# Fewer scratch buffers for a casting DMA, and a reordered weight preparation, in a gated recurrence followed by a max-out layer

## The chip, the cores and the metric

The kernel runs on one core of one Trainium2 chip. The metric is the device time of one execution in microseconds (us). Times of one kernel agree within about 0.3% most of the time. A few executions are much longer; those are marked slow (over 1.5% above the fastest of the same kernel), and every comparison here uses the fast runs alone. A ratio is the mean time of one kernel's fast runs over the mean of the other's fast runs of the same rounds, so it is not quite the ratio of the medians that are quoted beside it.

Engines: PE is TensorE's matmuls, PEld its weight loads, DVE is VectorE, ACT is ScalarE, POOL is GpSimd, SP is SyncE. SPq is the queue in which SP issues DMAs.

## The reference

Two parts run one after the other. The first is a gated recurrence over time for 4 sequences of 6144 steps with 256 features:

```python
sig = 1.0 / (1.0 + np.exp(-f_logit))
f = lower_bound + (1.0 - lower_bound) * sig
h = 0
for t in range(S):
    h = f[:, t] * h + (1.0 - f[:, t]) * x[:, t]
    y[:, t] = h
```

The second takes the 24576 rows of `y` through a layer with two branches, 1024 hidden units each, and a maximum between them:

```python
h1 = y @ w1
h2 = y @ w2
out = np.maximum(h1, h2) @ w_out
```

## The kernel before

The kernel uses `max(h1, h2) = h1 + relu(h2 - h1)`. So the first layer is one product with the difference `wd = (w2 - w1)`, a relu, and the second layer adds `y @ (w1 @ w_out)`. The product `w1 @ w_out`, called `w13`, is made once at the start, for which `w1` has to be transposed on TensorE. All of it is scaled by `om = 1 - lower_bound`, because the kernel leaves that factor out of the recurrence.

Time is cut into 48 blocks of 512 steps. For each block the features must lie on the partitions, so the inputs are transposed. The first chunks are transposed on TensorE. From chunk 5 on (`f`) and 6 on (`x`) it is done by DMA: POOL issues a DMA that casts a chunk of 1024 steps from float32 in DRAM to a bfloat16 scratch buffer, also in DRAM, and SP issues a DMA transpose from there into SBUF.

```python
NSCR = 6
...
            elif by_xbar(c, s):
                scr = scratch[s][uses[s] % NSCR]
                uses[s] += 1
                nc.gpsimd.dma_start(out=scr..., in_=src...)      # cast, DRAM to DRAM
...
                nc.sync.dma_start_transpose(out=dst[:, :, 0:nt], in_=held[c, s][0:nt, :])
...
LEAD_FETCH = 10
LEAD_CROSS = 3
```

A cast may overwrite a scratch buffer only when the transpose that reads it is done, so the number of buffers is the number of casts per tensor that can run ahead. POOL has little else to do and runs ahead as far as it may.

The weights before (with cuts):

```python
        make_w1s(0); make_w1s(1)          # ACT: w1s = om * w1, four times 512 strided columns
        ...
        make_wd(0)                        # DVE: wd = om * w2 - w1s
        for fc in range(0, NQ):
            first_layer(0, fc)            # PE: dT = wd.T @ y; ACT: rt = relu(dT)
        ...
        make_wd(1)
        make_w1T(0); make_w1T(1)          # PE: transpose w1s; ACT: copy to w1T
        for fc in range(NQ, FC):
            first_layer(0, fc)
        make_w1T(2); make_w1T(3)
        make_w13()                        # PE: w1T.T @ w_out; ACT: copy
```

## Time and profile before

The median was 408.92 us in the rounds of the comparison (408.33 to 409.08). The numbers that matter:

| Reading | Value |
|---|---|
| span of the profiled execution | 405.9 us |
| PE busy | 388.1 us, 96% of the span |
| one block in the steady state | 7.82 us |
| all waits of PE | 11.5 us, six of them, in five groups |
| wait of PE in the middle of the work | 1.2 us, at 64 us |

The busy times are the first part of the page of the kernel before (busy us, share of the span, instructions):

```profile
PE 388.1 (96%) x2792; PEld 297.3 (73%) x2840; DVE 247.2 (61%) x345; ACT 273.4 (67%) x446; POOL 28.0 (7%) x59
```

The list of waits of PE in the kernel before (engine, line, what it waited for, microseconds in total, times, longest):

```profile
PE dT L313 <- DVE wd L273: 5.6, 2, 5.2
PE tT L155 <- DVE fn L101: 2.8, 1, 2.8
PE dT L392 <- DVE ident L381: 1.6, 1, 1.6
PE dT L313 <- ACT rt L321: 1.2, 1, 1.2
PE tT L155 <- DVE xn L101: 0.3, 1, 0.3
```

PE is the bound, and only the head of the kernel and one wait at 64 us leave it idle. The wait at 64 us is put down to `rt`, a relu on ACT. The timelines of the kernel before, first of the SP queue, then of ACT, then of PE, show what stood behind it (start, length, engine, line, operation, tiles, and in brackets the idle time before and what ended it):

```profile
30.05 13.82 SPq L365 DMA_DIRECT2D out_dram<-osb  x2
43.97 17.55 SPq L128 DMA_TRANSPOSE fT<-scr_0_90  x1
```

```profile
63.63 1.06 ACT L165 ACTIVATE u<-fT 128x1024 bf16<-128x1024 bf16 x1 [2.65 <-DMA fT<-scr_0_90]
```

```profile
65.22 0.59 PE L313 MATMUL dT<-y,wd 128*128 128x512 bf16 x2 [1.24 <-ACT rt L321]
```

The first DMA transpose sat 17.55 us in the SP queue and landed 19.6 us after its issue (the chain of waits has it as one piece from 43.97 us). ACT's sigmoid waited for it, the relus wait behind the sigmoid in ACT's queue, and PE waits for a relu to free a PSUM buffer.

The head is the other part. PE's timeline before, from the first layer of block 0 to the end of `w13`:

```profile
14.05 3.17 PE L313 MATMUL dT<-y,wd 128*128 128x512 bf16 x7 [0.42 <-DVE wd L273]
17.01 1.25 PE L287 MATMUL psO<-ident_f,w1s 128*128 128x128 f32 x8
18.09 1.98 PE L313 MATMUL dT<-y,wd 128*128 128x512 bf16 x8
19.91 1.03 PE L287 MATMUL psO<-ident_f,w1s 128*128 128x128 f32 x8
20.79 2.41 PE L297 MATMUL psO<-wob,w1T 128*128 128x256 bf16 x16
23.03 0.61 PE L155 MATMUL tT<-ident,fn 128*128 128x128 bf16 x8
```

What comes after 23.03 us is the transposes of block 1, so 23.0 us is the end of the head's weight work on PE.

### The profile page before, as it was taken

The numbers are of one execution on the slowest core, as the hardware profiler recorded it, in microseconds if no ns is written. First come the engines' busy times: TensorE is split into PE (matmuls) and PEld (weight loads), VectorE is DVE, ScalarE is ACT, GpSimd is POOL, SyncE is SP. The second block draws the span as 40 slices with busy tenths as digits, with TensorE's granted clock in tenths as the row PEclk, the third lists the DMA queues.
The fourth block names the chain that finished last, engine by engine and source line by source line (L and its number), as shares of the span: only waits on it lengthen the run. The fifth ranks groups of instructions, "written<-read, shape, count | busy, mean of one in ns | idle before, by whom it ended". The sixth has DMA issues, their size and how long they took to land.

```text
span 405.9 us, 7061 instructions
## 1 busy us (share of the span) xinstructions
PE 388.1 (96%) x2792; PEld 297.3 (73%) x2840; DVE 247.2 (61%) x345; ACT 273.4 (67%) x446; POOL 28.0 (7%) x59
## 2 busy tenths in 40 slices
PE   3699998999999999999999999999999999999996
PEld 2386776777777777777777777777777777777775
DVE  3557665676566567566656656756665665676641
ACT  2948655766766766676676677667667667766762
POOL 0721000000000000000000000000000000000000
PEclk9999999999999999999999999999999999999999
DMA  7999999997999999897997995989772662752212
GB/s 254 206 214 234 247 206 299 210 258 171 233 174 226 205 186 221 195 214 205 206 207 180 234 209 169 237 164 211 155 157 90 170 144 77 195 131 77 105 53 103
DMA packets 97568, 75.43 MB, mean 186 GB/s; under 512 B 87280, under 2 KB 87792, under 8 KB 96880
## 3 DMA queue, kind: packets, MB, share of 16 engines
q1 hardware_dynamic: 93984, 49.56, 47.7%
q0 software_dynamic: 3264, 25.17, 34.2%
q8 instruction: 22, 0.36, 0.4%
q10 hardware_dynamic: 288, 0.26, 0.2%
q14 instruction: 10, 0.08, 0.1%
HBM read 53.48 MB, written 46.66 MB: 247 GB/s over the span
## 4 chain that ended last, share of the span: by engine, by line
PE 82%; DMA 14%; issue 1%; SPq 0%; POOL 0%; ACT 0%; DVE 0%; ACTq 0%
PE psO L342 49%; PE dT L313 34%; DMA fT<-scr_0_90 5%; DMA scr_0_90<-in_f_logit_dram 4%; DMA scr_4_94<-in_f_logit_dram 3%; DMA w1n_118<-in_moe_w_dram 2%; DMA fn<-in_f_logit_dram 1%; POOL waited L269 0%; SPq L97 0%; ACT rt L321 0%; POOL wob L398 0%; SPq L380 0%; SPq L259 0%; DVE osb L351 0%; PE tT L155 0%
## 5 line engine op out<-in xcount | busy, mean ns | idle before, releaser
L321 ACT ACTIVATE rt<-dT 128x512 bf16<-128x512 f32 x384 | 223.3, 598 | 109.5 <-PE dT L313 93.4
L342 PE MATMUL psO<-wob,rt 128*128 128x256 bf16 x1536 | 229.1, 273 | 0.2
L313 PE MATMUL dT<-y,wd 128*128 128x512 bf16 x720 | 218.5, 382 | 6.9 <-DVE wd L273 5.6
L342 PEld LDWEIGHTS <-rt 128*128 128x128 bf16 x1536 | 170.0, 113 | 40.7
L362 DVE COPY osb<-psO 128x512 f32<-128x512 f32 x94 | 64.8, 691 | 76.2 <-PE psO L342 76.0
L208 DVE TENSOR_TENSOR_SCAN y<-ff,y,v 128x512 bf16<-128x512 bf16 x88 | 107.8, 1266 | 0.0
L313 PEld LDWEIGHTS <-wd 128*128 128x128 bf16 x768 | 73.9, 98 | 15.9 <-DVE wd L273 6.4
L342 PE MATMUL psO<-w_117,y 128*128 128x256 bf16 x384 | 73.3, 273 | 2.3
L342 PEld LDWEIGHTS <-y 128*128 128x128 bf16 x384 | 43.3, 113 | 41.0 <-issue 0.3
L195 DVE TENSOR_TENSOR v<-u,xT 128x1024 bf16<-128x1024 bf16 x40 | 27.7, 692 | 55.0 <-ACT u L165 55.0
L165 ACT ACTIVATE u<-fT 128x1024 bf16<-128x1024 bf16 x42 | 44.1, 1051 | 2.7 <-DMA fT<-scr_0_90 2.7
L184 DVE TENSOR_SCALAR ff<-u,nom 128x512 bf16<-128x512 bf16 x96 | 29.3, 347 | 0.0
L195 DVE TENSOR_TENSOR v<-u,tT 128x1024 bf16<-128x1024 bf16 x8 | 9.7, 1218 | 16.2 <-ACT u L165 14.9
L165 ACT ACTIVATE u<-tT 128x1024 bf16<-128x1024 bf16 x6 | 6.2, 1039 | 7.6 <-PE tT L155 7.5
L208 DVE TENSOR_TENSOR_SCAN y<-ff,v 128x512 bf16<-128x512 bf16 x8 | 9.3, 1206 | 0.0
L155 PE MATMUL tT<-ident,xn 128*128 128x128 bf16 x64 | 8.6, 230 | 0.3 <-DVE xn L101 0.3
L155 PE MATMUL tT<-ident,fn 128*128 128x128 bf16 x48 | 5.1, 234 | 2.8 <-DVE fn L101 2.8
L155 PEld LDWEIGHTS <-fn 128*128 128x128 bf16 x48 | 3.9, 105 | 3.5 <-DVE fn L101 3.1
L155 PEld LDWEIGHTS <-xn 128*128 128x128 bf16 x64 | 5.4, 103 | 0.6 <-DVE xn L101 0.6
L106 POOL DMA_DIRECT2D scr_0_90<-in_f_logit_dram x4 | 2.0, 496 | 50.0 <-DMA fT<-scr_0_90 49.4
L106 POOL DMA_DIRECT2D scr_2_92<-in_f_logit_dram x4 | 1.9, 487 | 37.0 <-DMA fT<-scr_2_92 36.2
L106 POOL DMA_DIRECT2D scr_1_91<-in_f_logit_dram x4 | 2.0, 495 | 36.4 <-DMA fT<-scr_1_91 35.8
(41 smaller groups left out, 49.4 us busy)
## 6 DMA issues: line engine op xcount, KB each, us to landing
out_dram<-osb SPq DMA_DIRECT2D x47, 512.0 KB, 3.6
scr_0_90<-in_f_logit_dram POOLq DMA_DIRECT2D x4, 512.0 KB, 6.9
scr_1_91<-in_f_logit_dram POOLq DMA_DIRECT2D x4, 512.0 KB, 6.2
scr_0_96<-in_x_dram POOLq DMA_DIRECT2D x4, 512.0 KB, 8.1
scr_2_92<-in_f_logit_dram POOLq DMA_DIRECT2D x4, 512.0 KB, 7.8
scr_1_97<-in_x_dram POOLq DMA_DIRECT2D x4, 512.0 KB, 8.4
scr_3_93<-in_f_logit_dram POOLq DMA_DIRECT2D x3, 512.0 KB, 6.7
scr_2_98<-in_x_dram POOLq DMA_DIRECT2D x3, 512.0 KB, 9.1
```

The costliest lines, as they stand in the source:

```text
L106: nc.gpsimd.dma_start(out=scr[0:nt, :].rearrange("(p i) d -> p (i d)", p=P), in_=src.rearrange("(p i) d -> p (i d)", p=P),)
L155: nc.tensor.transpose(dst, src, ident[:])
L165: nc.scalar.activation(out=like(u[:, :, 0:nb], src), in_=src, func=AF.Sigmoid, scale=-1.0)
L184: nc.vector.tensor_scalar(out=ff[:, h, 0:nb], in0=u[:, h, 0:nb], scalar1=nom[:, h : h + 1], scalar2=1.0, op0=ALU.mult, op1=ALU.add,)
L195: nc.vector.tensor_tensor(out=like(v[:, :, 0:nb], src), in0=like(u[:, :, 0:nb], src), in1=src, op=ALU.mult,)
L208: nc.vector.tensor_tensor_scan(out=y[:, h, 0:nb], data0=ff[:, h, 0:nb], data1=v[:, h, 0:nb], initial=init, op0=ALU.mult, op1=ALU.add,)
L313: nc.tensor.matmul(dT[:, 0:nb], lhsT=wd[:, kc, fc * P : (fc + 1) * P], rhs=y[:, kc, 0:nb], start=(kc == 0), stop=(kc == KC - 1),)
L321: nc.scalar.activation(out=rt[:, 0:nb], in_=dT[:, 0:nb], func=AF.Relu)
L342: nc.tensor.matmul(ps[:, r, :], lhsT=left, rhs=right, start=(s == 0 and (r == 0 or j == NBLK - 1)), stop=(s == n - 1 and (r == 1 or j == N ...
L362: nc.vector.tensor_copy(out=osb[:, 2 * g : 2 * g + 2, :], in_=ps[:])
```

## The change

The intent has three parts, which are named in what follows. The *queue part*: two scratch buffers per tensor and a shorter fetch lead, so that casts run at most two chunks ahead. The *weights part*: raw `w1` is transposed as soon as it lands, DVE makes the difference and evicts the transposes, ACT only scales. The *hoist*: in block 2 all of `second_layer(1)` goes ahead of the first layer. The core of the diff, with cuts and added comments:

```diff
-    NSCR = 6
+    NSCR = 2
-    LEAD_FETCH = 10
+    LEAD_FETCH = 7
...
+            ahead("cross", cross, j + LEAD_CROSS)
             ahead("fetch", fetch, j + LEAD_FETCH)
-            ahead("cross", cross, j + LEAD_CROSS)
...
+    def make_wd(k):
+        nc.vector.tensor_tensor(out=pair(wdf, k), in0=half(w2n, g)[:, :, qs],
+            in1=half(w1n, g)[:, :, qs], op=ALU.subtract)
         for kc in range(KC):
+            nc.scalar.mul(wd[:, kc, cols], wdf[:, kc, cols], om[:, kc : kc + 1])
...
+        pts = [turn_w1(0), turn_w1(1)]    # PE transposes of raw w1
+        make_wd(0)
         make_wd(1)
+        for fc in range(0, 2):
+            first_layer(0, fc)
+        keep_w1T(0, pts[0])               # DVE evicts
+        make_wd(2)
...
+            if j == 2:
+                for fc in range(FC):
+                    second_layer(1, fc)
             for fc in range(FC):
                 if j < NBLK:
                     first_layer(j, fc)
-                second_layer(j - 1, fc)
+                if j > 2:
+                    second_layer(j - 1, fc)
```

Two smaller edits of the diff are not shown. As raw `w1` is transposed, `om` is multiplied in when ACT evicts `w13`. And the scans of block 2 now come after the first layer of block 1 instead of before it.

More of the change, by code (lines that the diff above doesn't have):

```diff
@@ L238 @@
     wob = wpool.tile([P, FC, D], BF16)
-    w1s = wpool.tile([P, KC, DFF], FP32)
+    wdf = wpool.tile([P, KC, DFF], FP32)
     wd = wpool.tile([P, KC, DFF], BF16)
@@ L262, in fetch_w, with pair, turn_w1 @@
             )
-    def make_w1s(g):
-        for kc in range(KC):
-            nc.scalar.mul(fcs(w1s, kc, g), half(w1n, g)[:, kc], om[:, kc : kc + 1])
     def pool_waits(t):
         nc.gpsimd.tensor_copy(out=waited[:], in_=t)
-    def make_wd(g):
-        for kc in range(KC):
-            nc.vector.scalar_tensor_tensor(
-                out=fcs(wd, kc, g),
-                in0=half(w2n, g)[:, kc],
-                scalar=om[:, kc : kc + 1],
-                in1=fcs(w1s, kc, g),
-                op0=ALU.mult,
-                op1=ALU.subtract,
-            )
-    def make_w1T(k):
+    def pair(w, k):
+        return w[:, :, 2 * k * P : 2 * k * P + 2 * P].rearrange(
+            "p kc (q m) -> p kc q m", q=2
+        )
+    def make_wd(k):
+        g, r = divmod(k, NQ // 2)
+        qs = slice(2 * r, 2 * r + 2)
+        nc.vector.tensor_tensor(
+            out=pair(wdf, k), in0=half(w2n, g)[:, :, qs], in1=half(w1n, g)[:, :, qs],
+            op=ALU.subtract,
+        )
+        cols = slice(2 * k * P, 2 * k * P + 2 * P)
+        for kc in range(KC):
+            nc.scalar.mul(wd[:, kc, cols], wdf[:, kc, cols], om[:, kc : kc + 1])
+    def turn_w1(k):
+        g, r = divmod(k, NQ // 2)
         pt = ps_o.tile([P, KC, 2, P], FP32, name="psO")
@@ L285, in make_w1T, with keep_w1T @@
             for q in range(2):
-                fc = 2 * k + q
                 nc.tensor.transpose(
-                    pt[:, kc, q, :], w1s[:, kc, fc * P : (fc + 1) * P], ident_f[:]
+                    pt[:, kc, q, :], half(w1n, g)[:, kc, 2 * r + q], ident_f[:]
                 )
+        return pt
+    def keep_w1T(k, pt):
         dst = w1T[:, 2 * k : 2 * k + 2, :].rearrange("p q (k d) -> p k q d", k=KC)
-        nc.scalar.copy(out=dst, in_=pt[:])
+        nc.vector.tensor_copy(out=dst, in_=pt[:])
     def make_w13():
@@ L303, in make_w13 @@
                 )
-            nc.scalar.copy(out=w13[:, kc, :], in_=psw[:, 0, :])
+            nc.scalar.mul(w13[:, kc, :], psw[:, 0, :], om[:, kc : kc + 1])
     rts = {}
@@ L394 @@
         recurrence(0)
-        make_w1s(0)
-        make_w1s(1)
         pool_waits(w1n[0][:, 0, 0:1])
@@ L402 @@
         pool_waits(w2n[1][:, 0, 0:1])
-        make_wd(0)
-        for fc in range(0, NQ):
-            first_layer(0, fc)
         fetch(1)
@@ L409 @@
         ahead("fetch", fetch, LEAD_FETCH)
+        pts = [turn_w1(0), turn_w1(1)]
+        make_wd(0)
         make_wd(1)
-        make_w1T(0)
-        make_w1T(1)
-        for fc in range(NQ, FC):
+        for fc in range(0, 2):
             first_layer(0, fc)
-        make_w1T(2)
-        make_w1T(3)
+        keep_w1T(0, pts[0])
+        make_wd(2)
+        for fc in range(2, 4):
+            first_layer(0, fc)
+        make_wd(3)
+        keep_w1T(1, pts[1])
+        pts = [turn_w1(2), turn_w1(3)]
+        for fc in range(4, 6):
+            first_layer(0, fc)
+        keep_w1T(2, pts[0])
+        for fc in range(6, 8):
+            first_layer(0, fc)
+        keep_w1T(3, pts[1])
         make_w13()
@@ L422 @@
         turn(turn_steps(2))
-        recurrence(2)
+        gate(2)
         for fc in range(FC):
             first_layer(1, fc)
+        for step in scan_steps(2):
+            step()
         turn(turn_steps(3))
```

## The prediction

> **What bounds the kernel now.** TensorE. The page gives PE 388.1 of 405.9 us busy, at a granted clock of 1.0; the chain of waits is 82% PE, and the list of waits shows only five waits of PE, 11.5 us in total, all in the first 14 us but for 1.2 us at 64 us, for `rt`. From about 65 us on, the timeline repeats every 7.82 us per block without a PE wait, and PE is busy 49.7 of 50 us in every later stretch, whether DMA share is above 1.0 (100-150 us) or 0.58 (300-350 us). So less DMA traffic can't speed up the middle. Only the head (first 65 us) can give.
>
> **What the change removes.**
> 1. *The 1.2 us wait at 64 us.* The first DMA transpose (`fT<-scr_0`) was issued at 44.0 us behind eleven casts that POOL had queued by 41.3 us; it landed 19.6 us later, where the median is about 6 us. ScalarE's sigmoid waited for it, and PE 1.2 us behind that. With two scratch buffers only three scratch casts (f, f, x) can be queued before that transpose, and as `second_layer(1)` moves ahead of block 2, the transpose is issued about 8 us earlier. It should land by about 46 us, long before use. Gain 1.2 us.
> 2. *Weight preparation on ScalarE.* Before: four scalings of 1.15 us, four `w1T` evictions of 0.6 us and the relus are in one ScalarE queue, so PE, although "busy", takes from 13.0 to 23.0 us for work that I estimate at 7.5 us. After: `w1` is transposed as it lands (10 us), in PE's idle time; DVE subtracts; ScalarE only scales eight contiguous 256-column pieces (about 0.37 us each, from the 256-column eviction), and DVE evicts `w1T` (0.69 us each). I walk this through as: subtractions at 11.9, 12.9, 14.5, 15.6 us; relus end at 20.7; `w13` done at 21.0 instead of 23.0. Gain about 2 us.
>
> **What it adds.** ScalarE in block 2 no longer has second-layer matmuls to hide behind: eight relus at 0.5 us plus a sigmoid of 1.0 us, against 4.4 us of PE; and `y3` is scanned only after `second_layer(1)`. Estimated new stall 0.3 to 0.8 us. Transposes and subtraction read raw `w1` with a stride of four floats.
>
> **What it doesn't change.** The order in the SP queue is the same, and in the steady state each cast already waits for a transpose; a chunk lasts 15.6 us, against a cast of 6 to 9 us and a transpose of 4 to 7 us. Two buffers suffice; I expect no PE wait after 65 us.
>
> **Sum.** 409.0 - 1.2 - 2.0 - 0.2 (block 2's wait for `y2`) + 0.6 = 406.2 us. Range 404.2 to 409.0. Faster by over 2%: 0.03; within 2%: 0.94; slower: 0.03.
>
> **What would show it.** `w13`'s eviction ends near 21 us; the first transpose lands before 50 us; no PE wait on `rt` at 64 us; the period stays 7.82 us; casts run until about 340 us instead of 275; DMA share falls in 20-60 us and rises after 300 us.
>
> **What would make it wrong.** The subtraction's cost. The Trainium skill ("SBUF - State Buffer", the note on SBUF cachelines) says that accesses that cross to a new 16-byte line each time pay a penalty. The trace agrees: ScalarE's strided `w1s` takes 1.15 us for 512 columns against 0.6 for the contiguous relu, and DVE's `wd` with one strided input 1.1 us. I assume 1.07 us for two strided inputs. If it is near 2.1, `w13` is done only at about 24 us and the total is about 409. A cast that lands late behind two buffers would add waits on the sigmoid every 15.6 us, and make it slower.

## The result, and the profile after

The changed kernel took 406.11 us in the median (405.53 to 406.53, 4 runs), against 408.92 us. The ratio of the fast runs is 0.9933, with a 95% interval of 0.9916 to 0.9950. The span of the profiled execution is 404.0 us.

The list of waits of PE after:

```profile
PE tT L155 <- DVE fn L101: 3.0, 1, 3.0
PE psO L288 <- DMA w1n_110<-in_moe_w_dram: 2.2, 1, 2.2
PE dT L396 <- DVE ident L385: 1.6, 1, 1.6
PE dT L317 <- ACT wd L281: 1.5, 1, 1.5
PE dT L317 <- ACT rt L325: 0.3, 1, 0.3
PE tT L155 <- DVE xn L101: 0.3, 1, 0.3
```

The wait of 1.2 us on `rt` is gone; a wait of 0.35 us on `rt` at 42 us is new. The timelines of the changed kernel, of the SP queue, POOL, ACT and PE in turn, show both:

```profile
29.11 9.43 SPq L369 DMA_DIRECT2D out_dram<-osb  x2
38.64 3.75 SPq L128 DMA_TRANSPOSE fT<-scr_0_90  x1
```

```profile
45.09 0.49 POOL L106 DMA_DIRECT2D scr_0_90<-in_f_logit_dram  x1 [22.81 <-DMA fT<-scr_0_90]
```

```profile
60.29 1.05 ACT L165 ACTIVATE u<-fT 128x1024 bf16<-128x1024 bf16 x1
```

```profile
42.12 0.59 PE L317 MATMUL dT<-y,wd 128*128 128x512 bf16 x2 [0.35 <-ACT rt L325]
```

The first transpose is issued at 38.6 us and has landed by 45.1 us, when POOL, which waited for it, goes on with the next cast. The sigmoid at 60.3 us has no wait before it.

The head after:

```profile
13.65 3.59 PE L317 MATMUL dT<-y,wd 128*128 128x512 bf16 x8 [1.53 <-ACT wd L281]
17.04 1.74 PE L288 MATMUL psO<-ident_f,w1n_111 128*128 128x128 f32 x8
18.61 1.89 PE L317 MATMUL dT<-y,wd 128*128 128x512 bf16 x7
20.34 1.91 PE L301 MATMUL psO<-wob,w1T 128*128 128x256 bf16 x16
22.08 0.61 PE L155 MATMUL tT<-ident,fn 128*128 128x128 bf16 x8
```

Block 1's transposes start at 22.08 us, 0.95 us earlier than before (how much of such a difference is chance is shown below, where the clock at the start is looked at). Beyond 66 us nothing changed for PE: the block still lasts 7.82 us, although DMA's share between 300 and 350 us rose from 0.58 to 0.94, because the last cast is now issued at 335 us instead of 275.

### The profile page after: what moved, and what is told of

Read it like the earlier page. It is cut to its first block, busy times and chain, and to the rows that moved or that the text cites. A ratio compares the mean times of both kernels' runs of the same rounds, so it can differ in the third digit from the quotient of the medians.

```text
span 404.0 us, 7074 instructions
## 1 busy us (share of the span) xinstructions
PE 388.9 (96%) x2792; PEld 298.6 (74%) x2840; DVE 249.6 (62%) x349; ACT 270.0 (67%) x446; POOL 28.1 (7%) x59
## 4 chain that ended last, share of the span: by engine, by line
PE 94%; DVE 1%; DMA 1%; issue 1%; ACT 1%; SPq 0%; DVEq 0%
PE psO L346 54%; PE dT L317 38%; PE tT L155 1%; DMA x_124<-in_x_dram 1%; ACT rt L325 1%; PE psO L301 0%; PE psO L288 0%; DVE y L208 0%; DVE v L195 0%; ACT u L165 0%; DVE wdf L275 0%; DVE xn L101 0%; DVE ff L184 0%; ACT wd L281 0%; SPq L97 0%
## 5 line engine op out<-in xcount | busy, mean ns | idle before, releaser
L106 POOL DMA_DIRECT2D scr_0_90<-in_f_logit_dram x11 | 5.4, 490 | 142.5 <-DMA fT<-scr_0_90 142.0
L106 POOL DMA_DIRECT2D scr_1_91<-in_f_logit_dram x10 | 4.9, 489 | 127.1 <-DMA fT<-scr_1_91 126.6
L281 ACT ACTIVATE wd<-wdf,om 128x256 bf16<-128x256 f32 x8 | 3.6, 502 | 5.4 <-DVE wdf L275 5.4
```

The lines of the kernel that those rows point to most:

```text
L106: nc.gpsimd.dma_start(out=scr[0:nt, :].rearrange("(p i) d -> p (i d)", p=P), in_=src.rearrange("(p i) d -> p (i d)", p=P),)
L281: nc.scalar.mul(wd[:, kc, cols], wdf[:, kc, cols], om[:, kc : kc + 1])
```

## The experiments

Eleven kernels ran, all with a correct result. Each row gives the median, the range of its runs, and the ratio to the kernel before of the same rounds.

| Label | Parts | Median us | Lowest to highest | Ratio (95%) |
|---|---|---|---|---|
| e6_control | the kernel before | 407.94 | 407.74 to 408.89 | 0.9994 (0.9980 to 1.0009) |
| e1_queue | queue | 406.70 | 406.37 to 407.66 | 0.9965 (0.9949 to 0.9980) |
| e2_weights | weights | 420.07 | 409.66 to 438.91 | 1.0054 (1.0032 to 1.0077) |
| e5_hoist | hoist | 408.58 | 407.55 to 408.86 | 1.0007 (0.9994 to 1.0020) |
| e3_noqueue | weights, hoist | 411.46 | 410.40 to 456.86 | 1.0074 (1.0051 to 1.0097) |
| e4_nohoist | queue, weights | 405.43 | 405.06 to 405.57 | 0.9925 (0.9912 to 0.9938) |
| e12_after | all three | 405.68 | 405.42 to 406.75 | 0.9937 (0.9921 to 0.9952) |
| e7_contig | queue, weights, contiguous | 404.57 | 404.39 to 405.45 | 0.9917 (0.9903 to 0.9931) |
| e9_all | and more reordering | 405.50 | 404.83 to 406.22 | 0.9936 (0.9923 to 0.9949) |
| e10_warm | e7 and dummy matmuls | 404.06 | 404.03 to 404.17 | 0.9895 (0.9876 to 0.9913) |
| e11_warm_all | e9 and dummy matmuls | 404.15 | 403.79 to 404.50 | 0.9896 (0.9879 to 0.9912) |

The medians of e2 and e3 include slow runs; their ratios don't. e5_hoist, e6_control, e7_contig and e9_all ran on another chip than the other seven; across the two, the ratios are the better comparison.

### The queue part alone: e1_queue

```diff
 # the kernel before
-    NSCR = 6
+    NSCR = 2
-    LEAD_FETCH = 10
+    LEAD_FETCH = 7
+            ahead("cross", cross, j + LEAD_CROSS)
             ahead("fetch", fetch, j + LEAD_FETCH)
-            ahead("cross", cross, j + LEAD_CROSS)
```

> The kernel before with the queue part alone: two scratch buffers, fetch lead 7, transposes issued ahead of casts. Theory A (the backlog of eleven casts slows the first transpose): it lands within about 10 us of its issue at 44 us instead of 19.6, PE's wait at 64 us is gone, w13 is still evicted at about 23.6 us: 1.2 us faster or somewhat more if the timed runs wait longer than the profiled one (409.0 to about 407.5). Rival B (the first transpose is slow because it is issued late, behind the output of block 1, and not because of the backlog): it stays slow and PE still waits about 1 us at 64 us; no gain.

The ratio is 0.9965, or 1.4 us of 408. The transpose is still issued at 43.68 us, as late as before, but it leaves the SP queue after 2.66 us instead of 17.55, no transpose of this run takes longer than 7.1 us to land, and PE has no wait after 20 us:

```profile
43.68 2.66 SPq L128 DMA_TRANSPOSE fT<-scr  x1
```

So the backlog of casts, and not the late issue, made the first transpose slow. Rival B falls. The three edits of the queue part were not run one by one; what is shown is that fewer casts under way help, not which of the lines does it. In the changed kernel POOL's wait of 22.81 us for the transpose that frees its scratch buffer, shown above, speaks for the number of buffers.

### The hoist alone, and the change without the queue part: e5_hoist and e3_noqueue

e5_hoist is the kernel before with the hoist's lines of the diff; e3_noqueue is the changed kernel with `NSCR = 6`, `LEAD_FETCH = 10` and the old order of the two `ahead` calls.

> The kernel before with the second_layer(1) hoist alone (six buffers, old weight preparation). Theory A: block 2 takes 0.3 us longer, the first transpose is issued about 5 us earlier (39 instead of 44 us) but lands, as before, at about 63.5 us, when the backlog of casts is gone; PE's wait stays about 1 us: total between 0 and 0.7 us slower than before. Rival B (issue time matters): the transpose lands before 50 us and the kernel is 1 us faster.

> The changed kernel with the queue part undone (six buffers, lead 10), so weights and the earlier second_layer(1). Theory A: the first transpose is issued at about 38.6 us, but into the backlog of eleven casts, and lands no sooner than about 60 us; some wait at 61 us stays, 0 to 2 us, so it is slower than the changed kernel by up to 2 us. Rival B (only the issue time matters): it lands before 48 us and the time equals the changed kernel, 406.1.

The SP queue in e5_hoist, then in e3_noqueue:

```profile
39.58 20.78 SPq L128 DMA_TRANSPOSE fT<-scr  x1
```

```profile
39.00 22.40 SPq L128 DMA_TRANSPOSE fT<-scr  x1
```

Issued 4.4 and 5.0 us earlier than before, the transpose takes 23.4 and 25.3 us to land instead of 19.6, and so lands at 63.0 and 64.3 us against 63.5. The issue time moves, the landing hardly does: it comes when the eleven casts are through (the last of them lands at 61.9 us in the kernel before, 60.5 in e5_hoist and 61.6 in e3_noqueue). That confirms the theory a second way. As forecast, the hoist alone gains nothing (1.0007). Its wait at 64 us was forecast at about 1 us, though, and is smaller in the trace:

```profile
64.70 0.59 PE L313 MATMUL dT<-y,wd 128*128 128x512 bf16 x2 [0.37 <-ACT rt L321]
```

In this run the transpose landed half a microsecond earlier, and PE came later by a wait of 0.35 us at 43 us, which the hoist costs.

But e3_noqueue is slower than its forecast. It was to be at most 2 us above the changed kernel; its ratio is 0.0141 above that kernel's 0.9933, or some 5.7 us of 408, and 0.74% above the kernel before. PE's wait accounts for part. Here is PE's timeline in e3_noqueue:

```profile
65.95 0.59 PE L317 MATMUL dT<-y,wd 128*128 128x512 bf16 x2 [2.19 <-ACT rt L325]
```

And the stretches after that wait, in the same trace (from:to in us, length, busy time of PE, PEld, DVE, ACT, POOL, then the granted clock, DMA share, GB/s):

```profile
66.00:67.00 1.00, 1.00 (x9) 0.77 (x9) 1.00 (x3) 1.00 (x3) 0.00 (x0) 1.00 1.25 279
67.00:70.50 3.50, 3.50 (x16) 2.01 (x15) 3.16 (x4) 1.47 (x3) 0.00 (x0) 0.52 1.26 221
...
71.00:72.00 1.00, 1.00 (x10) 0.77 (x9) 0.10 (x1) 0.58 (x1) 0.00 (x0) 1.00 1.55 328
```

After a wait of 2.19 us PE runs 3.5 us at a granted clock of 0.52, which costs about 1.7 us more than the wait itself (3.5 times 0.48). In the kernel before, the wait of 1.24 us had no such sequel; its clock column stays at 1.00 there. In the Trainium skill, "TensorE: Matmul & The Clock Gate", section "Why this matters for your kernels", the advice is no idle gap of PE above about 3 us; here a gap of 2.19 us was followed by the half clock. The length of the gap alone does not decide: in the profile of e2_weights, which is a slow run, three waits of 3.4 to 4.0 us came with a half clock, but one of 3.08 us did not. That wait, and the stretch after it:

```profile
186.72 0.38 PE L317 MATMUL dT<-y,wd 128*128 128x512 bf16 x1 [3.08 <-ACT rt L325]
186.80:190.00 3.20, 3.15 (x22) 2.37 (x23) 3.14 (x6) 2.53 (x5) 0.62 (x1) 1.00 1.65 390
```

What else decides was not tested.

The wait and the half-clock stretch together are 3.9 us. What separates e3_noqueue from the changed kernel in the profiled executions is 408.3 - 404.0 = 4.3 us, so they are most of it; the other 0.4 us is there by the end of the head (block 1's transposes start at 22.45 us against 22.08). The profiled run of e3_noqueue is the fastest of its fast ones. The others have mean clocks down to 0.992, against 0.996, so more of the half clock; that this makes the 5.7 us is argued, not shown.

### The weights part alone: e2_weights

e2_weights is the changed kernel with both the queue part and the hoist undone.

> The kernel before with the weight preparation alone (six buffers, block 2 interleaved). Theory A: w13 ends about 1 us earlier than before (22.1 against 23.0 us), but the first transpose is as late as before, relative to PE's work even more in the way, so the wait at 64 us grows by about what was gained in the head, to about 2 us: total within 0.3 us of before. If head and queue simply add, it is 1 us faster.

The forecast was a time within 0.3 us of before. It is slower by 0.54%, about 2.2 us. PE reaches the sigmoid's block 1 us earlier and finds the transpose still outstanding, and the fast runs have mean clocks of 0.992 to 0.996, where those of the kernel before have 0.998 to 1.0. So what the weights part gains is lost to the wait, and the clock takes more on top. The profile of this kernel fell in a slow run. It too has a wait at this place, of 3.38 us up to 66.14 us, and its clock record has the half clock from 65.56 to 68.97 us; that the fast runs are alike is argued from their clocks.

Three of its six runs were slow (428 to 439 us). So were one of e3_noqueue (457 us) and two of the kernel before (427 and 450 us). Of all runs of kernels with six buffers reported here, 6 of 47 were slow; of those with two buffers, none of 38. In the slow run that was profiled, the transposes never catch up while casts are in flight. A typical stretch of its SP queue, and one after the last cast:

```profile
166.75 10.14 SPq L128 DMA_TRANSPOSE fT<-scr  x1
176.98 7.71 SPq L128 DMA_TRANSPOSE xT<-scr  x1
184.78 1.01 SPq L369 DMA_DIRECT2D out_dram<-osb  x2
...
344.12 2.59 SPq L128 DMA_TRANSPOSE fT<-scr  x1
346.80 2.24 SPq L128 DMA_TRANSPOSE xT<-scr  x1
351.51 8.15 SPq L369 DMA_DIRECT2D out_dram<-osb  x2
```

Up to 330 us the SP queue holds one DMA after the other, without a pause for the output to become ready; afterwards it waits for outputs again, as in a fast run. Why one execution falls into this and another does not was not tested.

### The hoist's cost: e4_nohoist and e12_after

e4_nohoist is the changed kernel with the hoist's lines undone; e12_after is the changed kernel again, in other rounds.

> The changed kernel with the second_layer(1) hoist undone. The trace of the changed kernel shows block 2 taking 9.2 us (32.9 to 42.1) where it took 8.9 before, so the hoist costs about 0.3 us where it stands. Theory A: without backlog the transpose does not need the earlier issue, so this is 0.3 us faster than the changed kernel (405.8). Rival C (the hoist is needed): the first transpose, issued at 43 us, comes late and PE waits again at 61 us, so it is slower by 0.5 us or more.

> The changed kernel unchanged, in the same rounds as the others, to place the hoist's cost and its own spread. Expected 406.1, ratio 0.993; no run above 410, as for all kernels with two buffers so far. If one is, the outliers of 427 to 457 us are not tied to the six buffers.

e4_nohoist comes to 0.9925, the changed kernel to 0.9933 and 0.9937. The intervals overlap, so the times alone do not decide that the hoist costs something; the traces show 0.35 us of wait on `rt` at 42 us with the hoist and none without. The transpose is issued at 42.84 us without the hoist, and PE still has no wait after it. So the hoist isn't needed, and rival C falls. e4_nohoist against e1_queue also prices the weights part where the queue part is in place: 0.9925 - 0.9965 is 0.40% of 408, or 1.6 us (1.3 us by the medians).

### Strided columns: e7_contig

The weights are read with a stride of four floats, which lets `w_out` be loaded in long pieces. Both orders were changed together, so the result stays right:

```diff
 # the changed kernel without the hoist
-        return w[g][:].rearrange("p kc (m q) -> p kc q m", q=NQ)
+        return w[g][:].rearrange("p kc (q m) -> p kc q m", q=NQ)
...
-            out=wob[:].rearrange("p (g q) c -> p g (q c)", g=NG),
-            in_=moe_w_out.rearrange("(g p q) c -> p g (q c)", g=NG, q=NQ),
+            out=wob[:],
+            in_=moe_w_out.rearrange("(n p) c -> p n c", p=P),
```

> The changed kernel without the hoist, with weights and w_out read in contiguous columns (result still right). Cacheline theory: each subtraction falls from 1.0 us to 0.6 to 0.7, each fp32 transpose from 0.22 to about 0.13 us of PE; the first layer of block 0 starts about 0.3 us earlier, ScalarE's wait behind the second group of transposes (0.4 us) goes: w13 ends 0.5 to 0.8 us earlier, total 404.8. Rival (fp32 itself costs this, not the stride): durations and total stay as without the hoist, 405.4.

The subtraction, in the list of instructions on its tile, in the changed kernel and then in e7_contig (nanoseconds, least, median, most):

```profile
L275 DVE TENSOR_TENSOR wdf<-w2n_112,w1n_110 x2: 1031/1046/1062, 12.0 to 13.0; 128x512 f32<-128x512 f32 x2
```

```profile
L275 DVE TENSOR_TENSOR wdf<-w2n,w1n x4: 669/684/687, 11.9 to 14.3; 128x512 f32<-128x512 f32 x4
```

For the subtraction the cacheline theory holds: 1.05 us falls to 0.68. (The skill's "VectorE: DVE Perf Modes", section "The TRN2 errata", has (N+151)/0.96 ns for a float32 `tensor_tensor` addition; for 512 that is 691 ns, and the contiguous subtraction, with a median of 684 ns, agrees.) For PE's transposes it fails: both groups still take 1.9 us in this run, no less than with the stride. The profiled execution is the slowest of this kernel's four, and block 1 starts in it at 22.22 us, no earlier than with the stride, though the first layer of block 0 starts 0.35 us earlier than in e4_nohoist (13.22 against 13.57 us), as forecast. The total, 404.57 us, is near the forecast, but its ratio is only 0.0008 below that of e4_nohoist, which is within the noise.

### TensorE starts at half rate: e9_all, e10_warm, e11_warm_all

If the stride doesn't slow the transposes, what does? The second group took 1.74 us in the changed kernel, but 1.43 in e2_weights. The group at 17 us of the kernel before, which is its first, took 1.25 us, but 1.92 in e6_control, which is the same kernel. And PE's weight loads for the first layer of block 0 start 0.43 us apart up to about 16.6 us, while the clock column shows 1.00. PEld's timeline in the kernel before:

```profile
14.45 0.15 PEld L313 LDWEIGHTS <-wd 128*128 128x128 bf16 x1 [0.28 <-issue]
14.88 0.15 PEld L313 LDWEIGHTS <-wd 128*128 128x128 bf16 x1 [0.28 <-issue]
15.30 0.15 PEld L313 LDWEIGHTS <-wd 128*128 128x128 bf16 x1 [0.28 <-issue]
```

The idle time before each is put down to nothing ("issue"), so no other engine holds them.

The record of the granted clock that is kept in each trace shows what the column hides. Its first entry is the moment of full clock, and whatever lies before it counts as 1.00, in the column and in the mean clocks above. This moment differs from run to run, and the group of transposes that starts near 17 us takes the longer the later it comes. With the new weights part it comes at 16.93 us in e12_after, 17.77 in e2_weights and 18.46 in the changed kernel, and the group takes 1.11, 1.43 and 1.74 us. In the kernel before and e6_control it comes at 17.43 and 19.07 us, and the group takes 1.25 and 1.92. So it is the clock and not the stride: with the full clock at 19.37 us in e3_noqueue (strided) and 19.17 in e7_contig (contiguous), the group takes 1.91 and 1.92 us.

e6_control was meant for the clock after the wait at 64 us:

> The kernel before, unchanged, for its own runs and clocks. In the weights-without-queue run the trace shows TensorE at half clock for about 3.4 us after a wait of 2.2 us. Theory A2 (a late first transpose costs twice: the wait, and beyond some length of it a half-clock stretch): some of the kernel's own runs show a mean clock of about 0.996 and are 1 to 2 us longer than those at 1.0. Rival: all runs show 1.0, and the timed median above the profiled run is only noise. Ratio to itself 1.000 within 0.2%.

The clocks of its five runs were all 1.0, and its wait at 64 us was 1.4 us. So Theory A2 is not borne out for the fast runs of the kernel before: no half clock follows its wait. What e6_control showed was the unsteady head: block 1 starts at 23.71 us in it, against 23.03 in the kernel before, which is the same program.

e9_all moves the third group of `w1` transposes ahead of the first layer and two relus of block 0 to DVE:

```diff
 # e7_contig
-        pts = [turn_w1(0), turn_w1(1)]
+        pts = [turn_w1(0), turn_w1(1), turn_w1(2)]
...
-            nc.scalar.activation(out=rt[:, 0:nb], in_=dT[:, 0:nb], func=AF.Relu)
+            if on_dve:                    # block 0, fc 5 and 7
+                nc.vector.tensor_scalar_max(out=rt[:, 0:nb], in0=dT[:, 0:nb], scalar1=0.0)
```

> As the contiguous one, and besides the third group of w1 transposes moved ahead of the first layer, into PE's idle time, and two of block 0's relus on DVE. If ScalarE's queue is what w13 waits for (21.2 us in the run without the hoist), w13 ends at 20.2 to 20.6 us and the total is 404.0 to 404.4. If something else ends last there, for instance w_out's arrival, it is 404.8 or above.

At 405.50 us it misses the 404.0 to 404.4 of its forecast and is no faster than e7_contig. By its forecast something other than ScalarE's queue would then end last; what, was not established. Then dummy matmuls were put into PE's idle time, between 2.7 us and the first `wd`; their result is never read:

```diff
 # e7_contig; e11_warm_all has this on e9_all, with 3 in the last group
+        keep_warm(14, ident[:])           # 14 matmuls of 128 columns
         turn(turn_steps(0))
+        keep_warm(6, ...)                 # 6 matmuls of 512 columns
...
         pts = [turn_w1(0), turn_w1(1)]
+        keep_warm(6, ...)
         make_wd(0)
```

> As the contiguous kernel, with dummy matmuls on data already there, in TensorE's idle time from 2.7 us until the first wd. In all runs so far the first layer's matmuls of block 0 start 0.43 us apart until about 17 us and 0.21 us apart later, whatever the clock column says. Theory (TensorE starts at half rate[...]): the first matmuls of block 0 are now 0.21 us apart where nothing else holds them, the second group of w1 transposes takes about 1.0 instead of 1.9 us, w13 ends 0.8 to 1.2 us earlier, total 403.4 to 404.0, and the spread of the runs narrows. Rival (the 0.43 us is ScalarE's pace, or the wait for wd): spacing and total stay, 404.6.

> The dummy matmuls together with the earlier third group of transposes and two relus on DVE. If, with TensorE at full rate, ScalarE's queue is what is left, this ends w13 another 0.3 to 0.7 us earlier than the warm contiguous one: 402.8 to 403.5. If it is not, no faster than that.

PE's timeline in e10_warm:

```profile
9.96 1.06 PE L288 MATMUL psO<-ident_f,w1n 128*128 128x128 f32 x8
...
15.32 1.04 PE L288 MATMUL psO<-ident_f,w1n 128*128 128x128 f32 x8
16.19 1.05 PE L317 MATMUL dT<-y,wd 128*128 128x512 bf16 x4
17.53 1.47 PE L317 MATMUL dT<-y,wd 128*128 128x512 bf16 x4 [0.29 <-ACT wd L281]
18.84 1.91 PE L301 MATMUL psO<-wob,w1T 128*128 128x256 bf16 x16
20.58 0.61 PE L155 MATMUL tT<-ident,fn 128*128 128x128 bf16 x8
```

Both groups of transposes take 1.05 us now, and block 1 starts at 20.58 us instead of 22.22 in e7_contig's profile. The clock record has the full clock at 9.35 us. So the half rate is real, and its end, which comes at a different moment in each run, made the head unsteady. Whether the times are steadier without it stays open: the four runs of e10_warm lie within 0.14 us and those of e7_contig within 1.06, but those of e11_warm_all, with dummy matmuls, within 0.71, and the five of e4_nohoist, without, within 0.51. The half rate at the start is what the Trainium skill says ("TensorE: Matmul & The Clock Gate", Part 1, "What's actually happening"): PE starts at half its clock, needs a busy window of about 3.4 us to leave it, and the window runs freely, so the moment varies. The traces agree: without dummy matmuls the full clock comes between 16.17 us (e9_all) and 19.37 (e3_noqueue), a wider spread than the page's plus or minus 500 ns (two runs of the kernel before are 1.64 us apart), and the half clock of e3_noqueue after its wait lasts 3.41 us in the clock record.

The gain over e7_contig is 0.5 us by the medians and 0.9 by the ratios (the two ran on different chips); 404.06 just misses the forecast of 403.4 to 404.0. e11_warm_all adds nothing to e10_warm, and misses its forecast of 402.8 to 403.5: ACT is idle for 0.96 us there before it evicts `w13`, waiting for PE, so ACT's queue is no longer what is last. e10_warm beats both the kernel before (ratio 0.9895) and the changed kernel (404.06 against 405.68 us of e12_after).

## Why the prediction was right or wrong

**The total** was right: 406.2 us forecast, 406.11 measured. That it came within 0.1 us is in part luck, as errors of the terms cancel: the queue part gave somewhat more than its 1.2 us (1.4) and the weights part less than its 2.0 (1.6).

**The bound** was right. Only the head and the wait at 64 us could give, and the period of 7.82 us did not change.

**The wait at 64 us, 1.2 us**: right, in cause and size. e1_queue measures 1.4 us for it; the first transpose landed at 45 us, where "by about 46 us" was written. But it names two reasons, and only one counts. The earlier issue ("about 8 us" forecast, 5.3 measured) does nothing while the backlog is there, as e5_hoist and e3_noqueue show, and is not needed without it, as e4_nohoist shows.

**The weights part, "about 2 us"**: the mechanism was right, the size too large. In the profiled executions PE leaves the head 0.95 us earlier (22.08 against 23.03), and `w13`'s last eviction ends at 22.8 us (22.29 plus 0.48), where 21.0 was forecast. Pairs of profiles in which the full clock comes at about the same moment give 0.9 us (e1_queue and e12_after) and 1.3 (e6_control and e3_noqueue). From the times of e4_nohoist and e1_queue the part is worth 1.6 us by the ratios and 1.3 by the medians. Two things were off in the walk-through. A scaling of 256 columns took 0.50 us, not 0.37; the relus ended at 21.3 us, not 20.7. And PE's half rate is missing from it. The second group of transposes took 1.74 us, in front of the fifth of block 0's eight first-layer pieces, because PE was still at half rate for most of it. The estimate of 7.5 us for PE's own work holds at full rate only: two halves of the first layer at 1.8 us, two groups of transposes at 0.9 and 1.7 us for `w13` make 7.1. So part of the ten microseconds that the prediction put down to ScalarE's queue was PE's own slowness: in e10_warm, at full rate and with contiguous columns, the head ends 1.5 us earlier still, at 20.58.

**Block 2, 0.6 us lost and 0.2 gained**: the loss was there, but smaller, and the gain was not. The wait on `rt` was 0.35 us, and block 2 lasts 9.22 us (32.90 to 42.12) instead of 8.88 (33.83 to 42.71). From block 1's transposes to block 2's first layer PE takes 10.80 us before (23.03 to 33.83) and 10.82 in e4_nohoist (21.88 to 32.70), so no wait for `y2` went away.

**The subtraction** at 1.07 us: right, 1.05 measured, and for the stated reason, as e7_contig shows. The comparison that the prediction gives for it, a scaling from SBUF against a relu from PSUM, is not of like with like; e7_contig's is.

**Two buffers suffice**: right. PE has no wait after 66 us in any profiled run with two buffers, and the last cast at 335 us (340 forecast).

**What the prediction did not see**: the parts don't add. The weights part alone makes the kernel slower by 0.54%, because what it gains in the head becomes waiting for the first transpose, and in e3_noqueue a wait of 2.2 us was followed by 3.5 us at half clock. Only with the queue part is it a gain. The sum came out right because both parts were there.

## What to carry to other kernels

A prefetch queue that may run far ahead can delay the one transfer that is needed next; bound its depth by what the consumer needs, and look for the first urgent transfer behind the backlog. Speeding up the head of a kernel is worth nothing while something later waits on a transfer with a fixed arrival, and a wait of a few microseconds on PE can cost nearly as much again in clock (2.2 us and 1.7 here). Try dummy matmuls in TensorE's idle time before its first real work (0.5 to 0.9 us here), and judge its rate by the distance of its matmuls rather than by the clock column alone.

## What the Trainium skill lacked or had wrong

- "TensorE: Matmul & The Clock Gate", section "Why this matters for your kernels": it warns of idle gaps above about 3 us. Here a wait of 2.19 us was followed by 3.5 us at a granted clock of 0.52, while one of 3.08 us in e2_weights was not, nor were those of 1.24 and 1.4 us.
- The same page, Part 1, has the half rate at the start right, and it warns that single records of the clock can be unreliable, but not that a profile's clock column may show full clock before the first record: the column shows 1.00 from 13 to 17 us while 512-column matmuls are 0.43 us apart, and 0.21 us or so once warm (six weight loads in 1.18 us from 19.10 us on in e6_control, where the first record is at 19.07).
- "SBUF - State Buffer", the note on cachelines, gives no size for the penalty on VectorE or TensorE: two float32 inputs with a stride of 16 bytes made a 512-column subtraction 1.05 us instead of 0.68. PE's second group of float32 transposes took 1.11 us with the stride (e12_after) and 1.04 without (e10_warm), with PE at full rate.
- No page has what a DMA transpose costs behind casts on another queue: 19.6 to 25.3 us behind a backlog of eleven casts of 512 KB each written, against a median of about 5 us.
